# Two of four first groups as chunk pairs of one batch, with token pairs in a row, on one Trainium2 core

## The chip, the cores and the metric

The kernel runs on one core of a Trainium2 chip. The metric is the device time of one execution in microseconds; lower is better. The kernel before has a median of 182.35 us over three runs. The core has a matrix engine (PE), a vector engine (DVE), an activation engine (ACT), a general engine (POOL) and an engine that issues DMAs (SP). Each runs its own instructions in the order in which the program gives them; semaphores hold an instruction back until its operands are there and its output buffer is free.

## What is computed

A linear attention with a decaying state, followed by an MLP. r, k and v have shape 4 x 8 x 768 x 48 (batch, head, token, dimension).

```python
state = np.zeros((B, H, D, D), dtype=np.float32)
for t in range(S):
    cur = np.einsum('bhd,bhe->bhde', u[None] * kt, vt)
    y[:, :, t] = np.einsum('bhd,bhde->bhe', rt, state + cur)
    state = w[None, :, :, None] * state + np.einsum('bhd,bhe->bhde', kt, vt)

x = np.ascontiguousarray(attn_out.transpose(0, 2, 1, 3)).reshape(B * S, H * D)
h = x @ w_in                      # 3072 x 384 by 384 x 2048
g = np.where(h >= 1, h, np.where(h <= -1, 0.0, (h + 1) ** 2 / 4))
out = g @ w_out                   # 3072 x 2048 by 2048 x 384
```

## The kernel before

The tokens of a batch are cut into six chunks of 128. A **unit** is one chunk of one batch: 128 tokens on 128 partitions, with 8 heads of 48 columns. A **group** is two units, 256 tokens; there are 12 groups, numbered chunk by chunk: group 0 holds chunk 0 of batches 0 and 1, group 1 chunk 0 of batches 2 and 3, group 2 chunk 1 of batches 0 and 1, and so on. Unit n is half j of group g, with n = 2g + j.

Within a chunk the recurrence is written with matrices. Each step has a name, and the profile shows its tiles:

- load, loadV: SP loads R, K and VF from DRAM, one row of 48 floats (192 B) for each token and head. For groups 0 and 1 each unit is loaded and worked on by itself (span, NSPLIT = 2), later groups whole.
- Rs = R * Wup and Ks = K * Wdn (L300) scale by powers of w; the tables Wup and Wdn are made by ACT from wb, which is log w spread over the partitions by a matmul of PE (bcw, L225). V is VF in bf16 (ACT).
- KU = K * u (L310), RKU = R * KU (L317), usum sums RKU over a head into diag (L325, DVE), V2 = V * diag (L333). Each of these products runs on DVE or POOL, as the order says.
- T turns Ks and Rs for groups 0 to 2 on PE, TT copies the result from PSUM; from group 3 on KRT does it by a DMA on SP's queue (L362).
- A = Ks by Rs for each head on PE (L370), AT is A times a triangular mask (L375, DVE), Y = AT by V plus the turned R by the state (L395, L400), y = Y + V2 (L414, DVE).
- Sp = Ks by V (L386); Tm and decay (L422, L424, L429) bring the state one chunk further, sbf makes its bf16 copy. Y of a chunk needs the state behind the chunk ahead.
- X and xT turn y for the MLP: on PE for groups 0 to 2, by DMA later.
- mm1 (L466) gives hp, a quarter q of the 2048 columns for 256 tokens at a time: a block of 12 matmuls. relu and square (ACT), gate (L484, DVE) make gt. mm2 (L494) adds four matmuls of 384 columns for a quarter and a unit. o copies the result, out stores it.

w_in comes in four DMAs from POOL's queue, w_out in four. PSUM has three large buffers h0 to h2, which T, A and hp share, and two small ones for Sp, Y, X and op. A buffer number stands behind the colon of each token.

The order of everything is the string ORDER, written out by hand: tokens like `Ks.0.0@D:0` (step, group, half, engine, buffer), which the last loop of the kernel turns into instructions one by one. So ORDER sets the order on every engine's queue and on SP's DMA queue. `~4` puts four matmuls with zeros ahead of a step. 18 such matmuls stand at the start.

Of the kernel before, what the change touches and what calls it, by code (L numbers as in the profile page):

```python
# [28 lines left out]

ORDER = """  # L30
warm.18 lw bcu:0 u_bc@A load.K.0.0:0 bcw:1 load.R.0.0:0 wcol:0 KU.0.0@P:0 Wup load.K.0.1 Rs.0.0@D:0 Wdn loadV.0.0:0
V.0.0@A:0 Ks.0.0@D:0 load.R.0.1 load.K.1.0:1 wCm RKU.0.0@P:0 load.R.1.0:1 Ks.0.1@D Rs.0.1@D loadV.0.1 KU.1.0@D:1
KU.0.1@P Sp.0:1~4 load.K.1.1 T.0:0 T.1:1 Tm.0 TT.0@A:0 usum.0.0:0 load.R.1.1 V.0.1@A loadV.1.0:1 Ks.1.0@D:1 RKU.0.1@P
A.0:2~3 Rs.1.0@P:1 RKU.1.0@P:1 AT.0.0:0 load.K.2.0:2 V2.0.0@P:0 T.2:0~1 usum.0.1 Sp.1:0 Y.0:1 usum.1.0:1 y.0:0
Ks.1.1@P TT.2@A:1 TT.1@A:2 KU.1.1@D A.2:2~6 V.1.0@A:1 Rs.1.1@P A.1:0~4 Tm.1 load.R.2.0:2 V2.1.0@D:1 X.0:1 AT.2.0:1
sbf.0@A Sp.2:0 Tm.2 xT.0@A:0 loadV.1.1 AT.1.0:2 Ks.2.0@D:2 sbf.1@A T.3:1 load.K.3.0:0 TT.3@A:0 V.1.1@A Y.2:1~7 A.3:2~3
Sp.3:0 RKU.1.1@P Tm.3 V2.0.1@P Rs.2.0@P:2 y.2:1 T.4:1~12 Y.1:0 loadV.2.0:0 TT.4@D:1 w_in.0 T.5:0 load.R.3.0:0
V.2.0@A:2 X.2:1 xT.2@A:1 TT.5@D:2 y.1:2 A.4:1 w_in.1 usum.1.1 w_in.2 A.5:0 sbf.2@A AT.4.0:0 KU.2.0@P:0 V2.1.1@D
RKU.2.0@P:0 X.1:1~1 Ks.3.0@P:0 xT.1@A sbf.3@A AT.5.0:1 Sp.4:0 Sp.5:1 mm1.0.0.0:1~3 w_in.3 AT.3.0:2 mm1.0.0.1 Tm.4:0
mm1.0.1.0:0 relu.0.0:0 usum.2.0:0 Y.3:0 mm1.0.1.1 y.3:0 square.0.0:0 mm1.0.2.-1:2 Rs.3.0@P:0 Tm.5:1 relu.0.1:1  # L40
V2.2.0@P:0 KU.3.0@P:1 decay.4 w_out.0 Y.5:0 square.0.1:1 Y.4:1 gate.0.0:0 KRT.K.3:0 relu.0.2:0 y.5:1 square.0.2:0
y.4:2 X.3:0 KRT.R.3:0 X.4:1 loadV.3.0:1 mm1.0.3.-1:1 gate.0.1:1 A.6:0 gate.0.2:2 xT.3@A X.5:0 xT.4@A:2 AT.6.0:2
relu.0.3:1 w_out.1 RKU.3.0@P:1 decay.5 A.7:2 AT.7.0:1 load.K.4.0:1 square.0.3:1 mm1.1.2.-1:0 gate.0.3:3 V.3.0@A:3
w_out.2 Sp.7:1 xT.5@A mm1.1.1.-1:2 Tm.7:0 usum.3.0:1 V2.3.0@P:1 relu.1.2:0 Sp.6:0 square.1.2:0 Y.6:1 sbf.5@A
# [519 lines left out]
```

## Time and profile before

| | us |
|---|---|
| median of 3 runs | 182.35 (181.99 to 184.2) |
| the profiled execution | 183.03 |
| its span, first to last instruction | 181.3 |
| PE busy | 165.1 (91%) |
| DVE busy | 131.8 (73%) |
| ACT busy | 132.9 (73%) |
| POOL busy | 119.3 (66%) |

The profile is of one execution. Busy times of different engines lie beside each other, so they don't add up to the span. PE's busy time is modelled at its ends, since matmuls overlap. The profiled execution's own time is 1.7 us longer than its span; times within the trace count from the span's start. A wait is named by what ended last ahead of it.

### The profile page before, as it was taken

Reading aid. Unit: us, or ns where it says so; the run is one execution under the profiler, and the core shown is the slowest. Engines: PE = TensorE matmul, PEld = TensorE weight load, DVE = VectorE, ACT = ScalarE, POOL = GpSimd, SP = SyncE. Lnnn points to the kernel's source line nnn. Section 1 sums busy time; section 2 is a strip of 40 time slices with the busy share of each in tenths; the row PEclk is TensorE's granted clock in tenths of the full one; section 3 lists DMA queues with packets and bytes.
Section 4 is the critical chain, followed back from the end, with each engine's and each line's share of the span. In section 5 each row is a group of like instructions: output and inputs, shape, how many; then the busy total and the mean of one; then the engine's idle time right before and its main releaser. Section 6 shows DMA issues by size and latency. Waiting matters only on the chain.

```text
span 181.3 us, 4097 instructions
## 1 busy us (share of the span) xinstructions
PE 165.1 (91%) x1668; PEld 124.6 (69%) x1668; DVE 131.8 (73%) x158; ACT 132.9 (73%) x169; POOL 119.3 (66%) x93
## 2 busy tenths in 40 slices
PE   7879676879889999999999799997999999999992
PEld 5558565668666686787876676785777778767760
DVE  4599999989725798588978659978888654525751
ACT  3637535999967899797575986689975966889751
POOL 2778999994997699999995799999940000000000
PEclk9999999999999999999999999999999999999998
DMA  6999997999999999999999999999070602004022
GB/s 119 219 216 224 183 162 109 223 194 194 160 181 196 210 202 247 219 216 225 237 123 205 263 183 218 197 202 212 4 188 4 195 24 34 15 23 150 4 87 87
DMA packets 107623, 28.78 MB, mean 159 GB/s; under 512 B 100946, under 2 KB 107604, under 8 KB 107604
## 3 DMA queue, kind: packets, MB, share of 16 engines
q1 hardware_dynamic: 103888, 25.37, 70.3%
q0 software_dynamic: 3712, 3.15, 11.9%
q8 instruction: 13, 0.21, 0.5%
q14 instruction: 6, 0.05, 0.1%
q10 hardware_dynamic: 4, 0.00, 0.0%
HBM read 20.45 MB, written 4.72 MB: 139 GB/s over the span
## 4 chain that ended last, share of the span: by engine, by line
PE 56%; DMA 15%; POOL 15%; DVE 5%; ACT 4%; issue 3%; SPq 0%; DVEq 0%; POOLq 0%; ACTq 0%
PE op L494 26%; PE hp L466 22%; DMA K<-in_k_dram 6%; DMA w_out_sb<-in_moe_w_out_dram 4%; POOL Rs L300 4%; POOL Ks L300 3%; DMA RT<-Rs 2%; DMA VF<-in_v_dram 2%; POOL RKU L317 2%; POOL V L333 2%; PE A L370 2%; POOL w_in_sb L263 2%; PE Y L395 2%; PE Y L400 1%; ACT sq L479 1%
## 5 line engine op out<-in xcount | busy, mean ns | idle before, releaser
L484 DVE SCALAR_TENSOR_TENSOR gt<-sq,hp 128x1024 bf16<-128x1024 f32 x48 | 58.0, 1217 | 30.1 <-ACT sq L479 29.9
L466 PE MATMUL hp<-xT,w_in_sb 128*128 128x256 bf16 (+1 forms) x600 | 70.6, 268 | 2.0 <-DVE AT L375 1.4
L494 PE MATMUL op<-w_out_sb,gt 128*128 128x384 bf16 x384 | 70.1, 326 | 1.0 <-DMA w_out_sb<-in_moe_w_out_dram 1.0
L466 PEld LDWEIGHTS <-w_in_sb 128*128 128x128 bf16 x600 | 55.7, 98 | 11.4 <-issue 1.2
L474 ACT ACTIVATE pt<-hp 128x1024 f32<-128x1024 f32 x48 | 48.8, 1018 | 14.8 <-PE hp L466 14.8
L494 PEld LDWEIGHTS <-gt 128*128 128x128 bf16 x384 | 36.3, 98 | 21.6 <-issue 1.4
L479 ACT ACTIVATE sq<-pt 128x1024 f32<-128x1024 f32 x48 | 50.3, 1056 | 1.1
L375 DVE TENSOR_TENSOR AT<-A,umask 128x1024 bf16<-128x1024 f32 x24 | 28.7, 1217 | 1.8 <-PE A L370 1.7
L310 POOL TENSOR_TENSOR KU<-K,u_bc 128x768 f32<-128x768 f32 (+1 forms) x12 | 20.6, 1715 | 4.9 <-ACT u_bc L197 3.5
L317 POOL TENSOR_TENSOR RKU<-R,KU 128x768 f32<-128x768 f32 (+1 forms) x14 | 22.4, 1601 | 1.8 <-DVE KU L310 1.5
L300 POOL TENSOR_TENSOR Rs<-R,Wup 128x768 bf16<-128x768 f32 (+1 forms) x12 | 20.5, 1710 | 0.2
L333 POOL TENSOR_TENSOR V<-V,diag 128x768 f32<-128x768 bf16 (+1 forms) x12 | 17.0, 1419 | 4.8 <-ACT V L197 3.3
L300 POOL TENSOR_TENSOR Ks<-K,Wdn 128x768 bf16<-128x768 f32 (+1 forms) x10 | 17.6, 1764 | 2.3 <-PE hp L466 1.4
L429 POOL TENSOR_TENSOR state<-Tm,wCm 128x384 f32<-128x384 f32 x16 | 16.0, 1002 | 2.4 <-DVE Tm L422 2.4
L197 ACT COPY oo<-op 128x384 f32<-128x384 f32 x20 | 9.2, 474 | 8.8 <-PE op L494 8.6
L197 ACT CAST V<-VF 128x768 bf16<-128x768 f32 (+1 forms) x14 | 10.4, 741 | 7.0 <-DMA VF<-in_v_dram 7.0
L414 DVE TENSOR_TENSOR yy<-Y,V 128x384 bf16<-128x384 f32 x18 | 9.9, 555 | 4.2 <-PE Y L400 4.1
L400 PE MATMUL Y<-V,AT 128*128 128x48 bf16 x192 | 11.2, 185 | 1.6 <-DVE AT L375 0.8
L400 PEld LDWEIGHTS <-AT 128*128 128x128 bf16 x192 | 9.6, 97 | 3.6 <-issue 1.7
L325 DVE TENSOR_REDUCE diag<-RKU 128x16 f32<-128x768 f32 (+1 forms) x14 | 11.5, 828 | 0.6 <-POOL RKU L317 0.6
L422 DVE TENSOR_TENSOR Tm<-Sp,state 128x384 f32<-128x384 f32 x16 | 8.8, 552 | 3.1 <-PE Sp L386 2.9
L197 ACT CAST state_bf<-state 128x384 bf16<-128x384 f32 x20 | 9.8, 509 | 0.0
(70 smaller groups left out, 117.0 us busy)
## 6 DMA issues: line engine op xcount, KB each, us to landing
out_dram<-oo SPq DMA_DIRECT2D x11, 384.0 KB, 2.7
K<-in_k_dram SPq DMA_DIRECT2D x10, 384.0 KB, 5.1
R<-in_r_dram SPq DMA_DIRECT2D x10, 384.0 KB, 5.0
VF<-in_v_dram SPq DMA_DIRECT2D x10, 384.0 KB, 4.8
w_in_sb<-in_moe_w_in_dram POOLq DMA_DIRECT2D x4, 384.0 KB, 6.2
w_out_sb<-in_moe_w_out_dram POOLq DMA_DIRECT2D x4, 384.0 KB, 8.0
K<-in_k_dram SPq DMA_DIRECT2D x4, 192.0 KB, 3.6
R<-in_r_dram SPq DMA_DIRECT2D x4, 192.0 KB, 4.1
```

What stands on the lines that cost most here:

```text
L197: nc.scalar.copy(out, in_) if e == "A" else engines[e].tensor_copy(out, in_)
L300: engines[e].tensor_mul(of_unit(dst, j0, j1)[:, :, :, :D], of_unit(tiles[what, g], j0, j1), rep(tab, j1 - j0))
L310: engines[e].tensor_mul(of_unit(tiles["KU", g], j0, j1), of_unit(tiles["K", g], j0, j1), rep(u_bc, j1 - j0))
L317: engines[e].tensor_mul(of_unit(tiles["RKU", g], j0, j1), of_unit(tiles["R", g], j0, j1), of_unit(tiles["KU", g], j0, j1))
L333: engines[e].tensor_mul(tiles["V2", g][:, hs, :], tiles["V", g][:, hs, :], tiles["diag", g][:, hs].unsqueeze(2).to_broadcast([P, hs.stop - ...
L375: nc.vector.tensor_mul(t.rearrange("p i n t -> p (i n) t"), tiles.pop(("A", n)).rearrange("p i n t -> p (i n) t"), umask.unsqueeze(1).to_b ...
L400: nc.tensor.matmul(t[:, 2 * p + i, :], tiles["AT", n][:, i, p, :], tiles["V", g][:, j * H + 2 * p + i, :], start=(c == 0), stop=True, skip ...
L466: nc.tensor.matmul(hp[:, f, cols], w_in_sb[:, i, n0 : n0 + P], tiles["xT", g][:, units, i, :], start=(i == 0), stop=(i == nK - 1), skip_gr ...
L474: nc.scalar.activation(tiles["pt", g, q], tiles["hp", g, q], AF.Relu, bias=0.5, scale=0.5)
L479: nc.scalar.activation(tiles["sq", g, q], tiles.pop(("pt", g, q)), AF.Square, bias=0.0)
L484: nc.vector.scalar_tensor_tensor(out=gt, in0=tiles.pop(("sq", g, q)), scalar=1.0, in1=tiles.pop(("hp", g, q)), op0=ALU.min, op1=ALU.max)
L494: nc.tensor.matmul(tiles["op", g, j], tiles["gt", g, q][:, f, j * P : (j + 1) * P], w_out_sb[:, n, :], start=(n == 0), stop=(n == nF - 1),)
```

## The change

Groups 0 and 1 are formed in another way: group 0 is chunks 0 and 1 of batch 0, group 1 is chunks 0 and 1 of batch 1. Groups 2 and 3 are then chunks 0 and 1 of batches 2 and 3 (geo); from group 4 on all is as it was.

In groups 0 and 1 a partition holds a pair of neighbouring tokens, so that a row in DRAM is 96 floats (384 B); 64 partitions hold one chunk, 128 both. Each load takes four heads of the whole group (LSPLIT = 2), and the half j of a product or a load means four heads, not a unit. Tables with the powers for even and odd tokens (Wup2, Wdn2) and a mask for pairs (umask2) come in addition. A of such a group is made of matmuls over 64 x 64 tiles, 16 in place of 8 for a TT tile. Y of both units is made in one step (y_pair): for each pair of heads one matmul with the state and eight over tiles of 64 partitions, in two phases with a filler between them: 73 matmuls. Sp adds two matmuls over 64 partitions for a result. Y of group 0 now holds chunk 1, so it needs the state behind chunk 0.

w is spread over 128 partitions by its own DMA, and ACT takes the logarithm there; the matmul wb goes. w_in comes in two DMAs (W_IN = 2). ORDER is new throughout, engines and buffers of many steps with it: u_bc is copied by DVE, some of group 3's products move to DVE, some of the o copies too.

```diff
-NSPLIT = 2
+PAIRED = 2
+W_IN = 2
+LSPLIT = 2
...
-    nc.scalar.dma_start(out=w_row, in_=w.rearrange("(o h) d -> o (h d)", o=1))
+    nc.scalar.dma_start(out=flat(w_bc), in_=w.rearrange("(o h) d -> o (h d)", o=1).to_broadcast([P, DM]))
...
+    def geo(g):
+        return (g - 2, 2) if PAIRED == 2 and g < 4 else (g // BP, g % BP * UNITS)
...
-        nc.scalar.activation(lw_row[:, :, :D], w_row.rearrange("o (h d) -> o h d", h=H), AF.Ln, bias=0.0)
+        nc.scalar.activation(lw_bc[:, :, :D], w_bc, AF.Ln, bias=0.0)
...
+    def up2(e, bk, j):
+        nc.scalar.activation(Wup2[:, :, j, :], lw_bc[:, :, :D], AF.Exp, scale=up_col[:, j : j + 1], bias=0.0)
...
-        n = slice(i * DF // NQ, (i + 1) * DF // NQ)
+        n = slice(i * DF // W_IN, (i + 1) * DF // W_IN)
...
+        if g < PAIRED:
+            hs = slice(j * H // LSPLIT, (j + 1) * H // LSPLIT)
+            src = x[g, hs, : 2 * C, :].rearrange("h (t j) d -> t h (j d)", j=2)
+            nc.sync.dma_start(out=t.rearrange("p (h j) d -> p h (j d)", j=2)[:, hs], in_=src)
...
+        if n // UNITS < PAIRED:
+            t = tiles["TT", n]
+            for p in range(2):
+                for js in range(2):
+                    for i in range(2):
+                        rows = slice(i * HP, i * HP + D)
+                        for z in range(2):
+                            cz = slice(z * HP, (z + 1) * HP)
+                            nc.tensor.matmul(
+                                A2[cz, i, 2 * p + js, :], t[rows, NP + 2 * js + p, cz], t[rows, p : p + 3 : 2, cz], start=True, stop=True,
+                            )
+            return
...
+    def y_pair(bk, g):
+        t = psum(f"h{bk[0]}", [P, 2, 4 * P], F32, "Y")
...
+        for phase in range(2):
+            if phase:
+                nc.tensor.matmul(t[:, 0, 4 * P - 1 :], ident, ident[:, :1], start=True, stop=True, skip_group_check=True)
+            for p in range(NP):
+                hh, pp = divmod(p, 2)
+                jt = phase ^ 1
+                nc.tensor.matmul(
+                    flat(tiles["Y", 2 * g + jt][HP:, 2 * p : 2 * p + 2, :]), tiles["TT", 2 * g + hh][:, 2 * jt + pp, HP:],
+                    states_bf[g][:, p, :], start=True, stop=False, skip_group_check=True,
+                )
+                for i in range(2):
+                    for js in range(2):
+                        for z in range(2):
+                            jt, rows = phase ^ z, slice(z * HP, (z + 1) * HP)
+                            nc.tensor.matmul(
+                                tiles["Y", 2 * g + jt][rows, 2 * p + i, :], tiles["AT", 2 * g + hh][rows, i, 2 * pp + js, jt * HP : (jt + 1) * HP],
+                                V[rows, js * H + 2 * p + i, :], start=(js == 0 and z == 0), stop=(js == 1), skip_group_check=True,
+                            )
```

DVE's queue at its first products, behind the constants of the start, before. R_150 and K_146 are group 0's tiles, K_169 and R_176 group 1's:

```order
L300 TENSOR_TENSOR Rs_100<-R_150,Wup_120 128x8x48
L300 TENSOR_TENSOR Ks_97<-K_146,Wdn_121 128x8x48 x2
L300 TENSOR_TENSOR Rs_100<-R_150,Wup_120 128x8x48
L310 TENSOR_TENSOR KU_181<-K_169,u_bc_122 128x384
L424 TENSOR_TENSOR state_112<-Sp_184,wCm_109 128x384
L325 TENSOR_REDUCE diag_215<-RKU_174 128x8
L300 TENSOR_TENSOR Ks_98<-K_169,Wdn_121 128x8x48
L375 TENSOR_TENSOR AT_238<-A_223,umask_86 128x1024
```

The same place of DVE's queue with the change. K_149 and R_151 are group 0's tiles, K_180 group 1's:

```order
L211 COPY u_bc_129<-ub_155 128x384
L355 TENSOR_TENSOR KU_159<-K_149,u_bc_129 128x384
L364 TENSOR_TENSOR RKU_161<-R_151,KU_159 128x384
L372 TENSOR_REDUCE diag_177<-RKU_161 128x4x2
L340 TENSOR_TENSOR Rs_105<-R_151,Wup2_127 128x4x2x48
L340 TENSOR_TENSOR Ks_102<-K_149,Wdn2_128 128x4x2x48
L355 TENSOR_TENSOR KU_159<-K_149,u_bc_129 128x384
L355 TENSOR_TENSOR KU_185<-K_180,u_bc_129 128x384
L364 TENSOR_TENSOR RKU_161<-R_151,KU_159 128x384
L211 COPY TT_254<-T_230 128x1024
L532 TENSOR_TENSOR state_117<-Sp_240,wCm_114 128x384
L530 TENSOR_TENSOR Tm_274<-Sp_262,state_117 128x384
```

KU and RKU of group 0 come from POOL to DVE, two of its four Rs and Ks go to POOL, and one copy of TT and that of u_bc come in; between the first product and the first state there were five products, now there are seven.

POOL's queue from its last product of groups 0 and 1 to the last DMA of w_out, before. Tile R_311 is group 2's, K_344 and R_432 group 3's, K_698 group 4's:

```order
L300 TENSOR_TENSOR Rs_102<-R_311,Wup_120 128x16x48
L263 DMA w_in_sb_66<-in_moe_w_in_dram 128x3x512 x3
L310 TENSOR_TENSOR KU_470<-K_240,u_bc_122 128x768
L317 TENSOR_TENSOR RKU_473<-R_311,KU_470 128x768
L300 TENSOR_TENSOR Ks_97<-K_344,Wdn_121 128x16x48
L263 DMA w_in_sb_66<-in_moe_w_in_dram 128x3x512
L300 TENSOR_TENSOR Rs_100<-R_432,Wup_120 128x16x48
L333 TENSOR_TENSOR V2_588<-V_434,diag_543 128x768
L310 TENSOR_TENSOR KU_590<-K_344,u_bc_122 128x768
L429 TENSOR_TENSOR state_112<-Tm_526,wCm_109 128x384
L267 DMA w_out_sb_67<-in_moe_w_out_dram 128x4x384 x2
```

The same stretch with the change, from the last Rs of group 1. R_219 and K_180 are group 1's tiles, K_277 and R_279 group 2's, K_326 group 3's:

```order
L340 TENSOR_TENSOR Rs_106<-R_219,Wup2_127 128x4x2x48
L296 DMA w_in_sb_66<-in_moe_w_in_dram 128x3x1024
L343 TENSOR_TENSOR Ks_104<-K_277,Wdn_126 128x16x48
L343 TENSOR_TENSOR Rs_107<-R_279,Wup_125 128x16x48
L355 TENSOR_TENSOR KU_185<-K_180,u_bc_129 128x384
L364 TENSOR_TENSOR RKU_522<-R_219,KU_185 128x384
L357 TENSOR_TENSOR KU_621<-K_326,u_bc_129 128x768
L296 DMA w_in_sb_66<-in_moe_w_in_dram 128x3x1024
L357 TENSOR_TENSOR KU_644<-K_277,u_bc_129 128x768
L364 TENSOR_TENSOR RKU_646<-R_279,KU_644 128x768
L385 TENSOR_TENSOR V2_746<-V_460,diag_710 128x768
L300 DMA w_out_sb_67<-in_moe_w_out_dram 128x4x384
```

The first half of w_in is ahead of all products of group 2 now, and Ks and Rs of group 3 are gone from POOL's stretch; its last three DMAs of w_out follow two steps behind the first, where before two products, two states and one wait stood between them and the last.

310 lines of the change are left out of this document (181 added, 129 removed).

## The prediction

> **What bounds the kernel now.** The page's summary comes first: who is busy, and when.
>
> ```profile
> PE 165.1 (91%) x1668; PEld 124.6 (69%) x1668; DVE 131.8 (73%) x158; ACT 132.9 (73%) x169; POOL 119.3 (66%) x93
> PE   7879676879889999999999799997999999999992
> DVE  4599999989725798588978659978888654525751
> ```
>
> TensorE (PE) is full from about slice 12 on; DVE is full in slices 2 to 8, while PE is not. So the span has two parts with different limits. The table by stages, cut where the matmuls of the MLP begin (26.20) and where PE has its last wait on a weight load (55.7), says how much PE loses in each:
>
> ```profile
> core 0: us, PE busy (x) PEld busy (x) DVE busy (x) ACT busy (x) POOL busy (x), PEclk, DMA share, GB/s
> 6.78:26.20 19.42, 14.85 (x202) 11.65 (x203) 19.40 (x27) 10.75 (x20) 17.78 (x16) 1.00 1.08 198
> 26.20:41.10 14.90, 11.47 (x160) 9.68 (x158) 14.08 (x17) 11.38 (x14) 14.46 (x12) 1.00 1.08 175
> 41.10:55.70 14.60, 13.46 (x124) 10.14 (x123) 9.10 (x10) 12.86 (x15) 11.37 (x8) 1.00 1.19 178
> 55.70:177.70 122.00, 119.65 (x1164) 89.01 (x1162) 87.07 (x94) 94.57 (x117) 73.21 (x48) 1.00 0.73 150
> ```
>
> From 6.78 to 26.20 DVE is busy for 19.40 of 19.42 us: the head is DVE's. After 55.7 PE idles 2.35 of 122 us: that part is PE's own work, which this change hardly touches (12 groups of 48 + 32 large matmuls stay). What can move the end is how far PE has got when it becomes full, plus those 2.35 us, whose named waits are in the list of PE's waits behind 55 us:
>
> ```profile
> PE Sp L386 <- ACT oo L197: 1.0, 1, 1.0
> PE Y L395 <- ACT oo L197: 0.9, 1, 0.9
> PE A L370 <- DMA RT<-Rs: 0.3, 1, 0.3
> ```
>
> **The head after the change, step by step.** I walk DVE's new order with durations from DVE's and POOL's rows in order of time (start, length, engine and line):
>
> ```profile
> 6.78 1.15 DVE L300 TENSOR_TENSOR Rs<-R,Wup 128x384 bf16<-128x384 f32 x1 [3.65 <-ACT Wup L234]
> 7.85 2.61 DVE L300 TENSOR_TENSOR Ks<-K,Wdn 128x384 bf16<-128x384 f32 x2
> 11.65 0.55 DVE L310 TENSOR_TENSOR KU<-K,u_bc 128x384 f32<-128x384 f32 x1
> 12.12 0.55 DVE L424 TENSOR_TENSOR state<-Sp,wCm 128x384 f32<-128x384 f32 x1
> 12.59 0.54 DVE L325 TENSOR_REDUCE diag<-RKU 128x8 f32<-128x384 f32 x1
> 13.61 1.21 DVE L375 TENSOR_TENSOR AT<-A,umask 128x1024 bf16<-128x1024 f32 x1
> 22.65 1.27 DVE L197 COPY TT<-T 128x1024 bf16<-128x1024 bf16 x2
> ```
>
> ```profile
> 7.47 1.31 POOL L310 TENSOR_TENSOR KU<-K,u_bc 128x384 f32<-128x384 f32 x1
> 8.85 1.19 POOL L317 TENSOR_TENSOR RKU<-R,KU 128x384 f32<-128x384 f32 x1
> 12.28 1.00 POOL L317 TENSOR_TENSOR RKU<-R,KU 128x384 f32<-128x384 f32 x1 [0.96 <-DVE KU L310]
> ```
>
> A product of two SBUF operands over half a group (384 elements) takes DVE 0.5 us when POOL is idle (11.65) and 1.07 to 1.3 when POOL runs its own products beside it (6.78, 7.85); POOL goes from 1.00 to 1.2-1.3. Each op starts some 0.07 before the one ahead of it ends (11.65 + 0.55 against 12.12), so products that read PSUM and sums count 0.47 (state, Tm, y, diag) and 1.14 (AT). In the new order POOL is busy beside DVE from its first Ks on, so I take **1.15 us** for each such half product on DVE; the ends are 0.5 and 1.3. [...]
>
> The start of it:
>
> ```profile
> 3.23 1.61 PE L230 MATMUL ub<-u_row,ones 1*128 1x384 f32 x2
> 2.83 0.52 ACT L220 ACTIVATE lw_row<-w_row 1x384 f32<-1x384 f32 x1
> 6.16 0.58 ACT L234 ACTIVATE Wup<-wb,up_col 128x384 f32<-128x384 f32 x1 [0.80 <-PE wb L225]
> K<-in_k_dram SPq DMA_DIRECT2D x4, 192.0 KB, 3.6
> ```
>
> *w by its DMA.* It removes the broadcast matmul wb and adds 128 rows to the first load on ACT's queue, ahead of u_row. That costs between 0 and 1.0 us (one load of 196 KB more before u_row lands, at the 198 GB/s of the table's first row); I take 0.3, so ub ends at 5.15 and u_bc, now copied by DVE (0.5), at 5.65. ACT's lw, 2.83 before, then starts at about 3.4, and six tables follow it instead of two, 0.53 each: dn2 are ready at 5.0, up2 at 6.1, against 6.7 for the old Wup. POOL's first Ks runs at 5.0, against 7.85 on DVE. The table masks and columns (POOL, DVE) fit before 5 us, where both are idle.
>
> *DVE's order to the first y.* KU, RKU, Rs, Ks, KU, KU, RKU: 7 x 1.15, and a sum of 0.47: 5.65 + 8.5 = 14.2. Then a TT copy 0.6, the two state products 0.94, a sum 0.47, AT 1.14, V2 1.15, AT 1.14: 19.6. Group 0's Y needs that second AT. It is now one block of 73 matmuls (64 tiles of 64 rows, 8 with the state, 1 filler) where two units took 16. The rows of Y before:
>
> ```profile
> 14.90 0.52 PE L400 MATMUL Y<-V,AT 128*128 128x48 bf16 x8
> 22.31 0.36 PE L400 MATMUL Y<-V,AT 128*128 128x48 bf16 x8
> L400 PEld LDWEIGHTS <-AT 128*128 128x128 bf16 x192 | 9.6, 97 | 3.6 <-issue 1.7
> ```
>
> At 22.31 the next block starts 0.20 behind: 25 ns each; at 14.90, 0.35: 44 ns. If a tile costs as much, the block takes 1.8 to 3.2 us; if every weight load stands alone (97 ns), 7.1. I take **3.2**, the slower of the measured paces. So Y.0 runs from 19.6 to 22.8, DVE has Tm and AT (1.6) beside it and then waits 1.6; y, y, Tm, AT end at 25.4. Y.1 follows on PE (25.4 to 28.6) beside a sum, RKU, a sum and two V2 (about 4.1 us, two of them with POOL idle): 29.5, hidden. y.2 ends at 30.0, its transposes on PE at 30.2. In the new order of PE the first MLP matmul stands right behind them: it starts at **30.2 instead of 26.20**. The second A's and Y's of the head cost PE more matmuls (16 instead of 8 per A), but PE waits for DVE there.
>
> *w_in in halves, and DMA.* POOL reaches the first half behind seven half products (5.0 + 7 x 1.2 = 13.5), the second at about 22; before:
>
> ```profile
> 20.61 2.47 POOL L263 DMA_DIRECT2D w_in_sb<-in_moe_w_in_dram  x3
> w_in_sb<-in_moe_w_in_dram POOLq DMA_DIRECT2D x4, 384.0 KB, 6.2
> w_out_sb<-in_moe_w_out_dram POOLq DMA_DIRECT2D x4, 384.0 KB, 8.0
> 46.64 0.80 POOL L267 DMA_DIRECT2D w_out_sb<-in_moe_w_out_dram  x1
> ```
>
> Twice 6.2 us at most puts the halves at 26 and 34; the second is needed about 32 to 34 (third block of group 0), so it may cost nothing to 2 us, I take nothing since it is issued with the queue less full. The 384 B rows halve the packets of twelve loads; at 198 GB/s these loads take 1.0 us each, so this is worth 0 to 6 us of DMA, but in the head no step waits for a load, and I put it at zero. The bytes are the same.
>
> *From the first MLP matmul to 51 us.* DVE goes on: y.3, Tm, AT, AT, a sum (0.85), Ks of group 3 (1.8; 0.9 to 2.6), Tm, y, y: 37.3, then the first gate (1.13). Before, the first gate started here:
>
> ```profile
> 31.67 1.21 DVE L484 SCALAR_TENSOR_TENSOR gt<-sq,hp 128x1024 bf16<-128x1024 f32 x1
> 39.82 1.47 PE L466 MATMUL hp<-xT,w_in_sb 128*128 128x256 bf16 x12
> 45.72 0.81 PE L494 MATMUL op<-w_out_sb,gt 128*128 128x384 bf16 x4
> 46.37 1.47 PE L466 MATMUL hp<-xT,w_in_sb 128*128 128x256 bf16 x12
> 48.37 1.46 PE L494 MATMUL op<-w_out_sb,gt 128*128 128x384 bf16 x8 [0.53 <-DMA w_out_sb<-in_moe_w_out_dram]
> 54.23 1.46 PE L494 MATMUL op<-w_out_sb,gt 128*128 128x384 bf16 x8 [0.48 <-DMA w_out_sb<-in_moe_w_out_dram]
> ```
>
> Group 3's two A cost PE 0.55 (below); with its two Sp and two Y (8 and 24 matmuls at a like pace) they come to about 1.9:
>
> ```profile
> 62.45 0.55 PE A L370 x16
> ```
>
> Eight mm2 matmuls take 1.46 and four 0.81, so a block of mm2 counts 0.65 and one of hp 1.47 - 0.16 = 1.31. Three PSUM buffers hold hp, so the fourth hp block waits for the first gate: 38.5, the sixth ends at 42.4 (before: 41.1). From there the new order wins back: mm2 blocks stand at once between the hp blocks, with A, Sp and Y of group 3 put off by about 12 us of PE work, and all of w_out is issued by 42 instead of 46.64. w_out.0 goes out behind V2 of group 2 (its sum ends on DVE at 34.1, V2 takes 1.5) at 35.6 and lands by 41.8 at w_in's 6.2 (43.6 at 8.0, a stall of 1.2). PE then reaches nine hp blocks and eight mm2 blocks at 51.5: 42.4 + 3 x 1.31 + 8 x 0.65. Before, nine hp and two mm2 were done at 47.84, and group 3's 1.9 besides; six more mm2 (3.9), less that 1.9, and the wait of 0.53 make it 50.4. So PE is **1.1 us late** at 51.
>
> *Behind 51 us.* The second wait on w_out (0.48) goes. Of the 2.35 us of idle PE, the new order gives relief: counted in MLP work that is left behind them on PE, A of groups 7 to 11 stand 1 to 10 us later than before, while the loads of groups 3 to 6 stand where they stood. I take 1.9 of 2.35 as gone; the ends are 0 (a new wait of the same size, below) and 2.35. The tail is alike: six mm2 blocks still cover the last relu, square and gate.
>
> **Sum.** 181.3 + 1.1 - 0.5 - 1.9 = 180.0 us of span. The profiled execution took 183.03, 1.73 more than its span, and the median of the three runs, 182.35, is 0.68 below it: 180.0 + 1.73 - 0.68 = **181.0 us**. On its own this case spans 179 to 184: w_out late by 1.2, half products at 1.3 (1.7), no relief behind 51 us (1.9), w_in's second half late (2), not all at once; a Y of 1.8 us and the last 0.45 the other way.
>
> **Rivals.** *Faster: the shared head is cheaper.* If half products on DVE cost about 0.8, halfway to the free 0.5, the eleven of them give back 3.5 us, Y.0's wait stays, MLP starts near 26.7, and PE is 2.4 us early at 51: 181.3 - 2.4 - 0.5 - 1.9 = 176.5 of span, **177.5**. For it: at 11.65 and at the sums DVE is quick, and POOL pauses when it issues w_in. Against it: all four contended rows agree. Chance 0.27.
>
> *Slower: the block of Y.* At 97 ns per matmul Y takes 7.1 us. Y.0 keeps DVE waiting 3.9 longer, and Y.1 (29.3 to 36.4) ends 3.0 after DVE is ready: MLP starts at 37.1, and since PE has no slack behind that, the end comes 6.9 later: **187.9**. Up to 4.1 us (0.9 above my 3.2) only Y.0 counts, beyond it both; 2% slower is reached at about 6.1 us, 84 ns per matmul. For it: weight loads are 64 per block and each tile needs its own, and between state and tile matmuls the shape of the array changes 16 times. Against it: weight loads overlap in every Y before. [...] Chance 0.21.
>
> *The change does not reach the end.*
>
> ```profile
> 49.43 1.81 POOL L300 TENSOR_TENSOR Rs<-R,Wup 128x768 bf16<-128x768 f32 x1
> ```
>
> DVE now makes Rs of group 3 at about 45, and SP's queue stands behind that for the transpose, R of group 4 with it; POOL's Rs of group 4 then waits to about 51, where it stood before. Then the middle stalls as before and nothing is won there: 181.0 + 1.9 = 182.9, within the forecast's own range.
>
> **Chances.** A measurement of this kernel tells 2% (3.6 us) from no change: faster below 178.7 has 0.27, slower above 186.0 has 0.21, between them 0.52, where the forecast lies. The range leaves about a tenth out at each side: 176.3, a little under the faster rival, to 187.4, just short of the slower one.
>
> **What would show it.** First MLP matmul at 28 to 32 us; the first block of Y near 3 us; DVE's half products at 1.1 to 1.2; first gate at 36 to 39; no PE wait on w_out; PE idle behind 55 us under 1 us. If Y takes under 2 us and MLP starts before 27, the faster rival holds; if MLP starts behind 34, the slower one. I would be wrong altogether if a load, not DVE, ended the waits before 30 us.

## The result

The kernel after takes **190.54 us** (median of 4 runs, 190.4 to 190.79), the kernel before 182.66 on the same chip (4 runs, 181.99 to 184.2): ratio **1.042**, 95% interval 1.035 to 1.049. It is slower by about 8 us, where 181.0 was predicted and 187.4 was the upper end of the range. The profiled execution took 190.4 us, its span is 188.6. Ratios and their intervals leave out executions over 1.5% longer than the fastest of their kernel.

Two rows of busy tenths of the page after, in the same 40 slices as before, and the granted clock. PEclk is the share of its full clock that PE was granted; where the trace holds no record of it, the page counts it as full. In the kernel after the records begin at 33.50 us, in the kernel before at 16.03, so the digits ahead of that say nothing.

```profile
PE 173.0 (92%) x1796; PEld 132.0 (70%) x1796; DVE 143.8 (76%) x168; ACT 134.9 (72%) x171; POOL 115.0 (61%) x92
PE   4986359979899999999999999999999999999992
DVE  5699975998689899778977798798968777354640
PEclk9999999958999999999999999999999999999998
```

Counted from 0, PE is full from slice 11 on, and slices 3 to 5 stand at 6, 3 and 5, where they stood at 9, 6 and 7 before. PE's busy time grew by 7.9 us and DVE's by 12.0, though DVE has only ten instructions more. The table by stages, from 60 to 180 us (length; busy time and number of instructions of PE, PEld, DVE, ACT, POOL; granted clock, DMA share, GB/s), first of the kernel after, then of before:

```profile
60.00:180.00 120.00, 120.00 (x1214) 90.56 (x1213) 93.04 (x103) 99.22 (x122) 77.97 (x51) 1.00 0.79 159
```

```profile
60.00:180.00 120.00, 115.35 (x1134) 86.06 (x1132) 84.96 (x92) 91.65 (x114) 69.61 (x46) 1.00 0.72 149
```

Of the 4.65 us that PE lacks before, 2.3 are the end of its span, behind its last matmul; the rest are waits. After, PE does not wait at all behind 60 us, so the loss lies ahead of it. DVE's rows of the kernel after, in order of time (start, length, engine and line):

```profile
6.31 0.56 DVE L211 COPY u_bc<-ub 128x384 f32<-128x384 f32 x1 [2.94 <-PE ub L245]
7.50 1.24 DVE L364 TENSOR_TENSOR RKU<-R,KU 128x384 f32<-128x384 f32 x1
14.86 0.68 DVE L211 COPY TT<-T 128x1024 bf16<-128x1024 bf16 x1
18.17 6.16 DVE L383 TENSOR_TENSOR V<-V,diag 128x384 f32<-128x384 bf16 x1
24.26 1.21 DVE L439 TENSOR_TENSOR AT<-A,umask 128x1024 bf16<-128x1024 f32 x1
30.19 1.02 DVE L523 TENSOR_TENSOR y<-Y,V 128x384 bf16<-128x384 f32 x2 [3.13 <-issue]
34.24 3.97 DVE L383 TENSOR_TENSOR V<-V,diag 128x384 f32<-128x384 bf16 x2
38.31 1.02 DVE L523 TENSOR_TENSOR y<-Y,V 128x384 bf16<-128x384 f32 x2
```

The row at 18.17 is the heart of it: V2 of group 0's second half (V2.0.1), a product of 384 elements, stays on DVE for 6.16 us. The second AT of group 0, on which Y.0 waits, is behind it in DVE's queue. Beside it stood this on POOL:

```profile
16.68 1.83 POOL L343 TENSOR_TENSOR Ks<-K,Wdn 128x768 bf16<-128x768 f32 x1
18.46 1.81 POOL L343 TENSOR_TENSOR Rs<-R,Wup 128x768 bf16<-128x768 f32 x1
20.22 0.99 POOL L355 TENSOR_TENSOR KU<-K,u_bc 128x384 f32<-128x384 f32 x1
21.17 0.99 POOL L364 TENSOR_TENSOR RKU<-R,KU 128x384 f32<-128x384 f32 x1
22.12 1.79 POOL L357 TENSOR_TENSOR KU<-K,u_bc 128x768 f32<-128x768 f32 x1
33.89 1.79 POOL L357 TENSOR_TENSOR KU<-K,u_bc 128x768 f32<-128x768 f32 x1 [9.22 <-DVE RKU L364]
35.76 2.03 POOL L364 TENSOR_TENSOR RKU<-R,KU 128x768 f32<-128x768 f32 x1
```

V2 starts during POOL's Ks and ends at 24.33, 0.42 behind the end of POOL's fifth product; a free half product counts 0.47 (KU of the kernel before starts at 11.65, the product behind it at 12.12). So all but the end of its 6.16 us is waiting. None of the four products that POOL starts in that time is lengthened. The pair at 34.24 waits too, but for one product of POOL each. Then PE, from group 0's Y to the MLP:

```profile
25.52 0.24 PE L482 MATMUL Y<-state_bf,TT 128*64 128x96 bf16 x1 [4.88 <-DVE AT L439]
27.13 0.29 PE L482 MATMUL Y<-state_bf,TT 128*64 128x96 bf16 x1
27.35 0.41 PE L490 MATMUL Y<-V,AT 64*64 64x48 bf16 x8
33.72 0.23 PE L482 MATMUL Y<-state_bf,TT 128*64 128x96 bf16 x1
33.88 0.30 PE L490 MATMUL Y<-V,AT 64*64 64x48 bf16 x8
39.48 1.44 PE L572 MATMUL hp<-xT,w_in_sb 128*128 128x128 bf16 x12
44.20 0.83 PE L572 MATMUL hp<-xT,w_in_sb 128*128 128x128 bf16 x12
```

PE waits 4.88 us for the AT behind V2. The first Y runs at 0.55 us per pair of heads (27.13 to 27.69, where the next row stands), the second at 0.39 (33.72 to 34.11). **The MLP starts at 39.48** (26.20 before, 30.2 predicted), and its first blocks of 12 take 1.44 us where 0.83 is the full pace. The clock's records say why: 1.00 from 33.50 to 36.91, where the second Y runs, 0.50 from there to 43.74, and 1.00 again. The first Y lies ahead of the first record, at a pace that is slow too.

### The profile page after: what moved, and what is told of

It reads as the page before. It is cut to its first block, busy times and chain, and to the rows that moved or that the text cites. A ratio compares the mean times of both kernels' runs of the same rounds, so it can differ in the third digit from the quotient of the medians.

```text
span 188.6 us, 4363 instructions
## 1 busy us (share of the span) xinstructions
PE 173.0 (92%) x1796; PEld 132.0 (70%) x1796; DVE 143.8 (76%) x168; ACT 134.9 (72%) x171; POOL 115.0 (61%) x92
## 4 chain that ended last, share of the span: by engine, by line
PE 73%; DVE 14%; ACT 5%; issue 4%; DMA 2%; ACTq 0%; DVEq 0%
PE op L600 33%; PE hp L572 31%; DVE V L383 4%; PE A L431 3%; ACT pt L580 2%; ACT sq L585 2%; DVE AT L439 2%; PE Y L509 2%; DMA u_row<-in_u_dram 2%; PE Y L504 2%; DVE RKU L364 2%; DVE KU L355 2%; PE Sp L468 1%; DVE diag L372 1%; PE ub L245 1%
## 5 line engine op out<-in xcount | busy, mean ns | idle before, releaser
L572 PEld LDWEIGHTS <-w_in_sb 128*128 128x128 bf16 x600 | 57.6, 101 | 10.1 <-issue 1.2
L442 DVE TENSOR_TENSOR AT<-A,umask 128x1024 bf16<-128x1024 f32 x20 | 23.9, 1217 | 2.7 <-PE A L431 2.6
L343 POOL TENSOR_TENSOR Rs<-R,Wup 128x768 bf16<-128x768 f32 x9 | 16.4, 1819 | 12.5 <-DMA R<-in_r_dram 12.5
L357 POOL TENSOR_TENSOR KU<-K,u_bc 128x768 f32<-128x768 f32 x10 | 18.2, 1822 | 9.2 <-DVE RKU L364 9.2
L364 POOL TENSOR_TENSOR RKU<-R,KU 128x768 f32<-128x768 f32 (+1 forms) x11 | 19.5, 1773 | 0.2
L385 POOL TENSOR_TENSOR V<-V,diag 128x768 f32<-128x768 bf16 x9 | 13.9, 1544 | 7.8 <-DVE diag L374 7.8
L343 POOL TENSOR_TENSOR Ks<-K,Wdn 128x768 bf16<-128x768 f32 x9 | 16.4, 1818 | 3.2 <-DMA K<-in_k_dram 2.0
L211 ACT CAST V<-VF 128x768 bf16<-128x768 f32 (+1 forms) x14 | 10.2, 733 | 1.1 <-DMA VF<-in_v_dram 1.1
L383 DVE TENSOR_TENSOR V<-V,diag 128x384 f32<-128x384 bf16 x3 | 10.1, 3404 | 0.0
L509 PE MATMUL Y<-V,AT 128*128 128x48 bf16 x160 | 9.4, 183 | 0.0
L374 DVE TENSOR_REDUCE diag<-RKU 128x16 f32<-128x768 f32 x10 | 9.4, 943 | 0.0
## 6 DMA issues: line engine op xcount, KB each, us to landing
K<-in_k_dram SPq DMA_DIRECT2D x4, 192.0 KB, 5.4
R<-in_r_dram SPq DMA_DIRECT2D x4, 192.0 KB, 4.8
```

Of the source, the lines that this page charges most:

```text
L211: nc.scalar.copy(out, in_) if e == "A" else engines[e].tensor_copy(out, in_)
L343: engines[e].tensor_mul(of_unit(dst, 0, UNITS)[:, :, :, :D], of_unit(x, 0, UNITS), rep(tab, UNITS))
L357: engines[e].tensor_mul(of_unit(t, 0, UNITS), of_unit(x, 0, UNITS), rep(u_bc, UNITS))
L364: engines[e].tensor_mul(tiles["RKU", g][:, hs], tiles["R", g][:, hs], tiles["KU", g][:, hs])
L383: engines[e].tensor_mul(by_token(t, j), by_token(x, j), m)
L442: nc.vector.tensor_mul(*[y.rearrange("p i n t -> p (i n) t") for y in (t, x)], m)
```

## The experiments

The runs were made in several sets on different chips, and the kernel before itself took medians of 182.7 to 186.0 us in them, so times are compared by the ratio to the kernel before in the same set (with its 95% interval), and places by the trace. The kernel after was not run in most sets: a difference of 1% between ratios of two sets is not read. All edits are against the kernel after unless another run is named; where only tokens of ORDER are moved, the tokens are shown.

### V2 away from POOL's run

**V2.0.1 to POOL**, ahead of the run of products.

```diff
- V2.0.1@D
+ V2.0.1@P
```

> One letter: V2 of group 0's second heads goes from DVE to POOL. [...] Rival (the end is set behind the head, by the stretch without DMA at 26 to 43 us or by the clock of PE): the head shortens and the time stays within 1 us of 190.5.

Ratio 1.016 (1.011 to 1.021); span 186.1. POOL's row of V2 in this run:

```profile
17.15 0.84 POOL L383 TENSOR_TENSOR V<-V,diag 128x384 f32<-128x384 bf16 x1 [1.48 <-DVE diag L372]
```

The product takes 0.84 there, where the author expected 1.0 to 1.3, and the MLP starts at 34.49, 5.0 us earlier; about 34.5 was expected. The time, 187.4 us, lies above the 185 to 186.5 that were expected, but well below the two runs of the same set that leave V2.0.1 on DVE (190.1 and 192.6, below). So this one placement costs about 5 us at the MLP's start and over half of the 4.2% in time.

**All three V2 of groups 0 and 1 to POOL.**

```diff
- V2.0.1@D ... V2.1.0@D:1 ... V2.1.1@D
+ V2.0.1@P ... V2.1.0@P:1 ... V2.1.1@P
```

> All three V2 that DVE has in groups 0 and 1 go to POOL. [...] Rival (behind the head): within 1 us of 190.5.

Ratio 1.004 (0.997 to 1.011); span 185.0. The MLP's start does not move further (34.56), where 32 to 34 was expected. DVE's row of y.2:

```profile
33.16 1.02 DVE L523 TENSOR_TENSOR y<-Y,V 128x384 bf16<-128x384 f32 x2 [3.68 <-PE Y L490]
```

Now DVE waits for PE, whose second Y stands ahead of y.2 and ran at the slow pace (28.43 to 33.05; this trace's first record of the clock is at 37.29, with 1.00). From 15.6 to 42 PE rests only 0.4 and 0.6 us. The span fell by 1.1 all the same; 0.9 of it lies from 60 to 100 us, where PE was busy 39.54 of 40 us, against 38.61 in the run with one V2 moved. By its ratio this run is level with the kernel before.

**u loaded ahead of w's spread load**, V2 on DVE as in the kernel after.

```diff
-    nc.scalar.dma_start(out=flat(w_bc), ...)
     nc.scalar.dma_start(out=u_row, ...)
+    nc.scalar.dma_start(out=flat(w_bc), ...)
```

> The load of u goes ahead of the spread load of w on ACT's queue. If the spread load holds u back (u landed at 4.6 instead of before 3.2), ub starts at 3.2 to 3.5 and u_bc is there 1.2 us earlier; Ks and Rs still wait for w. [...] Rival (all of the head is a plain sum): 189.2 or less.

Ratio 1.011 (0.992 to 1.030), from only two executions, 191.39 and 188.80; MLP's start 39.41 in the first, which the trace shows. u_bc is copied at 4.71 (6.31 after), but in this execution V2 gives it all back. DVE's row of it:

```profile
17.15 7.12 DVE L383 TENSOR_TENSOR V<-V,diag 128x384 f32<-128x384 bf16 x1
```

V2 starts 1.0 earlier and ends at the same time, 0.42 behind the same product of POOL (22.06 to 23.85). Its length is not its own: it is the distance to the end of POOL's run, and that it would end there all the same was the author's expectation.

**A gap in POOL's run**: the second DMA of w_in between Ks and Rs of group 2.

```diff
- Rs.2.0@P:2 ... KU.3.0@P:0 w_in.1
+ w_in.1 Rs.2.0@P:2 ... KU.3.0@P:0
```

> w_in's second DMA is moved up on POOL, between Ks and Rs of group 2, so that POOL's run of five products has a gap of 0.8 us without an SBUF read at about 18.5; V2 stays on DVE. [...] Rival (V2 is slow by its own access pattern, or is served only behind the whole run): it still takes about 6 us, time 189.5 to 191.

Ratio 1.025 (1.010 to 1.039); MLP's start 40.38.

```profile
18.24 6.98 DVE L383 TENSOR_TENSOR V<-V,diag 128x384 f32<-128x384 bf16 x1
```

```profile
18.52 0.80 POOL L296 DMA_DIRECT2D w_in_sb<-in_moe_w_in_dram  x1
23.01 1.79 POOL L357 TENSOR_TENSOR KU<-K,u_bc 128x768 f32<-128x768 f32 x1
```

For 0.8 us POOL ran no product, and V2, which had been waiting since 18.24, did not use it. It ended 0.42 behind the last product again. The author's expectation that it gets in at such a gap, and ends at about 19, failed.

**The last product out of the run**: KU of group 3 behind RKU of group 2.

```diff
- KU.3.0@P:0 w_in.1 ... RKU.2.0@P:0
+ w_in.1 ... RKU.2.0@P:0 KU.3.0@P:0
```

> The product KU of group 3 on POOL is moved out of the run of five products, behind RKU of group 2; V2.0.1 stays on DVE. Starved to the end of the run: V2.0.1 starts at 18.2, POOL's run now ends with RKU of group 1's first chunk at 22.2, and V2 ends 0.4 behind that, at 22.6 (4.4 us instead of 6.2), so that the first MLP matmul comes 1.7 earlier, at 37.8. Tied to KU of group 3 or slow by its own addresses: V2 ends at 24.3 as before or later, or takes 6 us wherever POOL is.

Ratio 1.029 (1.019 to 1.038); MLP's start 37.67.

```profile
18.08 4.42 DVE L383 TENSOR_TENSOR V<-V,diag 128x384 f32<-128x384 bf16 x1
```

POOL's run ends with RKU at 22.08 now, and V2 at 22.50. With the run 1.8 us shorter V2 is 1.7 shorter, and the MLP starts 1.8 earlier: it is the run's end that V2 waited for, not that one product.

### Does the form of V2 decide?

In the kernel before such products got in behind one product of POOL, as the next two rows show (DVE's V2 ends 0.41 behind POOL's RKU); there V2 had two loops per operand, now it has three (4 x 2 x 48).

```profile
25.90 1.33 DVE L333 TENSOR_TENSOR V<-V,diag 128x384 f32<-128x384 bf16 x1
25.00 1.82 POOL L317 TENSOR_TENSOR RKU<-R,KU 128x768 f32<-128x768 f32 x1
```

Two runs cut V2.0.1 into two products of 192: by token (two loops left) and by heads (three left).

```diff
-            engines[e].tensor_mul(by_token(t, j), by_token(x, j), m)
+            if e == "D" and (g, j) == (0, 1):
+                for i in range(2):
+                    engines[e].tensor_mul(by_token(t, j)[:, :, i], by_token(x, j)[:, :, i], m[:, :, i])
+            else:
+                engines[e].tensor_mul(by_token(t, j), by_token(x, j), m)
```

By heads, i runs over the slices 0:2 and 2:4, and the operands are indexed `[:, i]`.

> V2.0.1 on DVE is issued as two products of 128x192 with three dimensions each (one per token of the pair) in the place of one of 128x384 with four. Starved by POOL's run, whatever the shape: the first half ends 0.2 to 0.3 behind KU of group 3 (24.2), the second 0.3 later; first MLP matmul at 39.5 as in the kernel after. Starved because of its four-dimensional addresses: each half gets in behind one product of POOL, both are done by 20.5 to 21, and the first MLP matmul is at 35.5 to 36.

> V2.0.1 on DVE again as two products of 128x192, but cut by heads, so that each keeps its four dimensions (in the run with three dimensions they were cut by token). Starved because of the four dimensions: the first waits for the end of POOL's run (KU of group 3, at 23.9), both are done at 24.3 to 24.5, first MLP matmul at 39.4. Starved because of the size of 384: each gets in behind one product of POOL, both done by 20.5 to 21, first MLP matmul at 35.5 to 36.

By token, the two products took 2.48 together and the MLP started at 35.73; by heads 6.24, and the ratio was 1.043 (1.033 to 1.052). First the one, then the other:

```profile
18.08 2.48 DVE L385 TENSOR_TENSOR V<-V,diag 128x192 f32<-128x192 bf16 x2
```

```profile
18.16 6.24 DVE L385 TENSOR_TENSOR V<-V,diag 128x192 f32<-128x192 bf16 x2
```

That looked like an answer. But by token the two executions took 187.9 and 192.0 us, and the profile is of the first. So the kernel after and both cuts were run again, six executions each.

> The kernel after, unchanged, in more executions. If every execution holds V2 up to the end of POOL's run: all times within about 1 us of each other, ratio to the kernel before 1.035 to 1.05. If the hold-up is a matter of chance in each execution: two clusters, 4 to 5 us apart (187 and 191).

> The run with V2.0.1 as two products cut by token, in more executions (the two so far took 187.9 and 192.0 us, and only the first has a profile, in which both halves got in). Form decides: nearly all executions near 188, 3 us below the kernel after. Chance in each execution: two clusters, 188 and 191 to 192, and the kernel cut by heads falls into the same two.

> The run with V2.0.1 as two products cut by heads, in more executions (191.1 and 192.7 so far, held up in the profile). Form decides: all near 191 to 192. Chance in each execution: some near 188.

The kernel after: 190.44 to 190.75 in all six, ratio 1.038 (1.034 to 1.042). By heads: 190.29 to 190.73, 1.037 (1.033 to 1.042). By token: 188.2, 189.0, and four of 190.6 to 191.3. The profile of one of these, the same program as the 2.48 above:

```profile
17.46 7.17 DVE L385 TENSOR_TENSOR V<-V,diag 128x192 f32<-128x192 bf16 x2
```

**The same program** let each half in behind one product of POOL in one execution and held both up to the end of the run (24.15) in another. So the form alone doesn't decide. By their times, the cut by token goes free more often than the other two (three of eight executions are below 190, against none of the ten of the kernel after and none of the eight cut by heads); only one of the three has a profile, and why is open.

### PE's pace

44 matmuls of zeros, ahead of the last Sp before Y.0, fill most of PE's wait (0.89 us of it is left).

```diff
- Sp.3:1 Y.0:0
+ Sp.3:1~44 Y.0:0
```

> 44 matmuls of zeros (128x128, 0.107 us each at half speed) fill PE's idle 20.6 to 25.4 ahead of Y.0; nothing else changes. [...] The pace of Y.0 is the tiles' own: 4.25 us again, and no gain.

If the clock sets it, then at about the pace of the second Y (0.40 per pair in the place of 0.55) Y.0 takes 3.3 us and not 4.25; for that case the author's estimate was a y.0 and an MLP 1 us earlier and a time 1 to 2 us below 190.5. Ratio 1.036 (1.026 to 1.046): no gain. Two pairs of heads of Y.0, early and late in it:

```profile
25.83 0.23 PE L482 MATMUL Y<-state_bf,TT 128*64 128x96 bf16 x1
25.99 0.31 PE L490 MATMUL Y<-V,AT 64*64 64x48 bf16 x8
27.76 0.29 PE L482 MATMUL Y<-state_bf,TT 128*64 128x96 bf16 x1
27.98 0.41 PE L490 MATMUL Y<-V,AT 64*64 64x48 bf16 x8
```

Y.0 begins at 0.39 per pair and falls back to 0.55 after 1.7 us, though PE never rests within it. So the slow pace is the clock's, and its records agree: 1.00 from 23.45 to 26.86, then 0.50 to 33.69. The 64 x 64 tiles, with the wait that was left, did not hold it up. y.0 came 0.6 earlier, and so did the MLP (38.91): filling the wait buys only half of what was expected, and in the ratio nothing of it is seen.

### Can the order be mended?

In the run with all V2 on POOL, PE's own order kept the MLP back: y.0 and y.1, all that its first block needs, were there at 26.4. **First MLP block ahead of Y.1** (with xT.1 and TT.5 moved up for it):

```diff
- Y.1:2 ... A.4:1 ... A.5:0 ... mm1.0.1.0:2 ... mm1.0.1.1 ... relu.0.1:0 ... square.0.1:0 ... gate.0.1:0
+ mm1.0.1.0:2 mm1.0.1.1 relu.0.1:0 square.0.1:0 Y.1:1 ... A.4:0 ... gate.0.1:0 y.2:2 ... A.5:1
```

> All three V2 of DVE in groups 0 and 1 go to POOL, as in the run where all were moved, and the first MLP block (mm1.0.1, both halves, 24 matmuls of 128x128) is put ahead of Y.1 on PE, whose inputs y.0 and y.1 are there at 26.3; its relu and square follow on ACT, its gate ahead of y.2 on DVE. If PE's order alone kept the MLP at 34.6: first MLP matmul at 28.3 to 28.6, PE at full speed from 31 on (full-array matmuls ahead of Y.1), the end 2 to 3.5 us ahead of the run with V2 moved: ratio to the kernel before 0.985 to 0.995. If the half of w_in is late (landing at 27 or later): first matmul up to 2 us later and no gain.

Ratio 1.005 (1.000 to 1.011), span 183.9.

```profile
28.23 2.35 PE L572 MATMUL hp<-xT,w_in_sb 128*128 128x128 bf16 x24
36.63 1.30 PE L572 MATMUL hp<-xT,w_in_sb 128*128 128x128 bf16 x12 [0.63 <-DVE AT L442]
```

The MLP starts 6.3 us earlier than in the run it builds on, and its span is only 1.1 less, where 2 to 3.5 were expected: PE had no gap there to fill, so the start of the MLP had stopped being the measure. What was won is pace (Y.1 at 0.39 per pair behind 24 full-size matmuls), and behind Y.1 it falls again (1.30; the clock's records go from 1.00 to 0.50 at 36.81).

**The same with u loaded first**, as above.

> The run with the first MLP block ahead of Y.1 (all V2 of groups 0 and 1 on POOL), and u loaded ahead of w's spread load. DVE's head is 1 us earlier, as in the run with u first, and no V2 on DVE eats it: Y.0 starts at 19.5 to 19.8 instead of 20.6, first MLP matmul at 27.2 to 27.8, the end 0.7 to 1 earlier: span 183, ratio to the kernel before 0.998 to 1.002. If POOL's head sets Y.0: no gain.

Ratio 1.004 (1.001 to 1.008), span 182.0, Y.0 from 19.56, MLP from 27.22. The profile shows 1.9 us less span, where 0.7 to 1 was expected, but its execution is the shortest of ten (183.8 to 186.1), and the ratio hardly moved. With no V2 on DVE, the 1 us of the head is kept.

**A second MLP block behind Y.1**, and w_in's second half earlier, on the run with u first:

```diff
- A.4:0 ... w_in.1 ... mm1.0.0.0:0 ... mm1.0.0.1
+ w_in.1 ... mm1.0.0.0:0 mm1.0.0.1 ... A.4:2
```

> The same with the second MLP block (mm1.0.0, both halves) directly behind Y.1 on PE, ahead of A.4, and the second half of w_in issued in POOL's wait ahead of V2.1. In the run with one block moved, PE's rate had fallen again after Y.1 (12 matmuls in 1.30 and 1.46 at 36.6 and 38.1): full-size matmuls behind Y.1 keep it up and take 0.83 each, and the wait of 0.63 ahead of them goes: 1.3 to 1.9 less, span 181 to 182, ratio 0.985 to 0.995, which would be below the kernel before. If A.4 and AT.4 behind it come late for the third block: PE waits there instead and the gain is below 0.5.

Ratio 1.013 (1.008 to 1.019), worse. In the profiled execution, the longest of six (188.0, the others 185.9 to 186.6), A.4 came late, and PE waited for DVE 1.4 and 1.8 us. Besides, the granted clock stood at 0.50 for 10.2 us between 32.38 and 46.03, where the run it builds on has 1.00 from 27.25 on, so the second block, put there to keep the pace up, ran at the slow one itself (24 matmuls in 2.74 us):

```profile
38.81 0.37 PE L509 MATMUL Y<-V,AT 128*128 128x48 bf16 x8 [1.41 <-DVE AT L442]
41.00 0.48 PE L509 MATMUL Y<-V,AT 128*128 128x48 bf16 x8 [1.82 <-DVE state L532]
41.30 2.74 PE L572 MATMUL hp<-xT,w_in_sb 128*128 128x256 bf16 x12
```

**Group 2's KU and RKU into POOL's wait, usum and Ks into DVE's**, on the run with u first:

```diff
- KU.3.0@P:0 w_in.1 ... KU.2.0@P:1 RKU.2.0@P:0 ... usum.2.0@D:0 Ks.3.0@D:0
+ KU.2.0@P:0 RKU.2.0@P:0 w_in.1 ... usum.2.0@D:0 Ks.3.0@D:0 ... KU.3.0@P:1
```

All of these but KU.3.0 now stand ahead of Y.1.

> The run with u first and the first MLP block ahead of Y.1, and group 2's KU and RKU put into POOL's wait ahead of V2.1 (24 to 28), with usum and Ks behind them in DVE's wait ahead of the first gate (29 to 33). PE's waits of that run between 34 and 41 (0.63, 0.30, 1.14 and 0.26 us, all for DVE) come from DVE's queue behind y.2: with two products of 0.95 fewer in it, 1.3 to 2 of these 2.3 us go, span 180 to 180.7, ratio to the kernel before 0.993 to 0.998. If PE then waits for something else (transposes' transfers, a fall of its clock): no gain, ratio 1.002 to 1.006.

Ratio 1.023 (1.016 to 1.030). The product that was moved into a wait was held up itself, by another run of POOL (V2, V2, KU and V2 from 28.14 to 32.98), 4.39 us for 0.95, and y.2, for which PE waits 2.8 us, stands behind it:

```profile
29.41 4.39 DVE L343 TENSOR_TENSOR Ks<-K,Wdn 128x768 bf16<-128x768 f32 x1
```

**That Ks as two products of 384**, a simpler form:

```diff
-            engines[e].tensor_mul(of_unit(dst, 0, UNITS)[:, :, :, :D], of_unit(x, 0, UNITS), rep(tab, UNITS))
+            n = 1 if (g, what) == (3, "K") else UNITS
+            for i in range(0, UNITS, n):
+                engines[e].tensor_mul(of_unit(dst, i, i + n)[:, :, :, :D], of_unit(x, i, i + n), rep(tab, n))
```

> The run with the head's new order, but Ks of group 3 on DVE as two products of 128x384 (one per unit) in the place of one of 128x768. In that run the one product (0.95 where POOL is idle) took 4.4 us, from 29.4 to 33.8, 0.8 behind the last of POOL's run of three products. Waiting is a matter of the product's form: each half gets in behind one product of POOL (ends at 31.6 and 33.4 at the latest, or 30.2 and 32), the first gate starts at 31.7 to 33.4 instead of 33.7, and PE's wait of 2.8 for y.2 becomes 0 to 2.4: span 181 to 183.5. POOL's run is waited for whatever the form: the gate at 33.7 to 33.9 again, span 184.

Ratio 1.039 (1.034 to 1.043), worse than whole. The group of the two, with least, median and greatest length in ns:

```profile
L345 DVE TENSOR_TENSOR Ks<-K,Wdn x2: 3347/4116/4886, 29.4 to 34.2; 128x384 bf16<-128x384 f32 x2
```

Each half was held up by itself, 4.9 and 3.3 us for about 0.43 (an estimate, half of the 0.86 from one start to the next of that Ks undisturbed, 42.84 to 43.70 in the kernel after): neither alternative of the expectation. The gate starts at 37.52.

**That Ks behind Tm of unit 4**, whole, away from this run of POOL:

```diff
- usum.2.0@D:0 Ks.3.0@D:0 ... Tm.4@D
+ usum.2.0@D:0 ... Tm.4@D Ks.3.0@D:0
```

> The same order with Ks of group 3 (one product) behind Tm of unit 4 on DVE, later than in every run so far, so that no DVE product of two SBUF operands stands beside POOL's run at 28 to 33. The gate starts at 31.5 to 32, y.2 at 33, PE's wait for it is 0 to 0.5 instead of 2.8, and the waits of 0.63 and 1.14 at 34 to 38 stay away: span 180.3 to 181.5, ratio to the kernel before 0.994 to 1.001. If Ks now waits for POOL's next run (RKU of group 3 at 34.7) and holds up y.4: span 182 to 183.

> The run with Ks of group 3 put back on DVE, in more executions. Its spans so far were 181.3, 181.3, 182.5 and, in the profiled one, 186.2, where that Ks took 5.9 us instead of 0.95. If the hold-up is a matter of each execution: executions near 183 and near 188 again; a profile of a short one shows Ks at 0.95 to 2 us, PE's wait for y.4 of 4.7 gone, and the first gate at 31. Ratio of the undisturbed runs to the kernel before 0.995 to 1.005.

The first profile is of an execution of 188.05 us, the longest of four (the others 183.0 to 184.3); the second of one of 183.82, among twelve from 182.3 to 184.7. DVE's row of Ks in the one, then in the other:

```profile
36.49 5.92 DVE L343 TENSOR_TENSOR Ks<-K,Wdn 128x768 bf16<-128x768 f32 x1
```

```profile
36.69 1.24 DVE L343 TENSOR_TENSOR Ks<-K,Wdn 128x768 bf16<-128x768 f32 x1
```

POOL's rows of the first:

```profile
34.74 1.81 POOL L364 TENSOR_TENSOR RKU<-R,KU 128x768 f32<-128x768 f32 x1
36.51 2.29 POOL L300 DMA_DIRECT2D w_out_sb<-in_moe_w_out_dram  x3
38.79 1.03 POOL L536 TENSOR_TENSOR state<-Tm,wCm 128x384 f32<-128x384 f32 x1
39.77 1.82 POOL L357 TENSOR_TENSOR KU<-K,u_bc 128x768 f32<-128x768 f32 x1
41.53 2.54 POOL L343 TENSOR_TENSOR Ks<-K,Wdn 128x768 bf16<-128x768 f32 x1
```

In both executions Ks starts at the same place, 0.06 and 0.08 ahead of the end of the same product. In the second it gets in at once, 0.3 longer than free, beside POOL's issuing of the same DMAs; in the first it stands through the 2.3 us in which POOL issues them and through two more products, and then POOL's next one is lengthened by 0.73. Again one program, two outcomes. Ratio 1.004 (0.997 to 1.012) at first, without the long execution, and **1.003 (0.998 to 1.007)** over the twelve executions of the second run: level with the kernel before. No run is faster than the kernel before.

## Why the prediction was wrong

The walk along DVE's queue was the right one, and its places can be compared step by step.

| step of the prediction | predicted | measured |
|---|---|---|
| u_bc ready | 5.65 | 6.87 |
| end of DVE's first products (start of the TT copy) | 14.2 | 14.86 |
| V2 of group 0's second half | 1.15 | 6.16 |
| second AT of group 0 ends | 19.6 | 25.47 |
| Y.0, to the start of y.0 | 3.2 | 4.7 |
| y.0 starts | 22.8 | 30.19 |
| y.2 ends | 30.0 | 38.9 |
| first MLP matmul | 30.2 | 39.48 |
| first gate | 37.3 | 46.09 |
| PE idle behind 55 us | 0.45 | 0 |

**The step that failed** is "I take 1.15 us for each such half product on DVE", with its end of 1.3, used for V2. Of the 9.3 us by which the MLP came late, 5.0 are that one product. The rows of the kernel before showed products alternating with POOL's, one against one, and I took that for a price per product. For the seven early ones it held: they ended 0.7 late, with u 1.2 late. At V2 POOL had five products ready in a row, and DVE waited for the rest of the first and all of the other four. The range did not hold this: its ends, 0.5 and 1.3, were lengths of single encounters, and no term depended on how long POOL's queue would run without a pause. The first run undoes the product's place and gets 5.0 us back; the one with KU moved shows that the run's end sets the length.

For single encounters the 1.15 and its end of 1.3 came near: products of DVE took 1.24 and 1.34 in the head of the kernel after. For V2 they did not, since behind the product of POOL that ran four more went ahead.

**The other terms.** *Loads of u and w.* "I take 0.3" for the row of u behind w's 128 rows was 1.2 too little at u_bc, and ACT's logarithm, put at 3.4, stands behind w's own load at 5.48; POOL's first Ks came at 7.30 instead of 5.0. *Y.* 4.7 instead of 3.2, of which about 1.2 is the clock by the pace of the second Y (eight pairs at 0.39 in the place of 0.55). The two paces that the prediction chose between, 44 ns a matmul at 14.90 and 25 at 22.31, lie on either side of 16.03, where the kernel before has its first record of the full clock; the new block takes 43 ns at the full clock and 61 at the slow one, so 3.2 met the full-clock length by luck. 64 weight loads don't cost 97 ns each, and no run shows a cost of the 16 changes between state and tile matmuls by themselves, so the slower rival (7.1 us, 187.9) came near the time by luck, through another cause. *Y.1 hidden* held: it ended at 36.6, ahead of DVE's pair of V2 at 38.2; that pair, each held up by one product, and the transposes at the slow pace make the last 1.9 us.

**What held, and how far.** Predicted was a start of the MLP 4.0 late and an end 1.3 early, so 5.3 won back; measured are 13.3 late and 7.3 late, so 6.0 won back, with no wait for w_out and none on PE behind 55 us. The size fits, and the relief shows in other runs too: from 55 to 175 us PE rests 2.32 before, 0 in the kernel after, and 0.39 in the run with the MLP block early and u first, whose MLP starts at 27.22. But it is not the same everywhere. In the run with V2.0.1 on POOL the MLP starts 4.9 us earlier than with u first and V2 on DVE, in the same set, and the span is only 3.5 shorter; PE rests 1.61 there, in the place of 0.60. The longest wait that has a name is one for a transposed Rs:

```profile
79.22 0.62 PE L431 MATMUL A<-RT,KT 48*128 48x128 bf16 x16 [0.84 <-DMA RT<-Rs]
```

So part of what the kernel after wins back may come with its late start; how much is not shown. The third rival had its condition right: SP's queue stood still behind Rs of group 3 from 45.1 to 57.3, and POOL waited 6.03 us for R of group 4, to 62.48. What should follow from it did not come: PE lost nothing by it. The rival of a cheaper head is out: it needed 0.8 us for a half product, and the seven took 1.07 each (6.87 to 14.86, less a sum of 0.47).

Two things I had no step for. With the MLP's start put right, PE is the limit from 15 us on, much of it at the slow pace (the kernel before has the full clock in its records from 16.03 to 179.87 without a break); that the mended orders stop at the time of the kernel before fits this, but no run separates it. And the predicted path had a second bound close behind the first: with all V2 on POOL, y.2 waits for PE's Y.1, which DVE had hidden.
